# Block-sparse attention with global keys, fused with a cosine MLP: blocks of 48 queries instead of 56, wrapped first keys, global rows gathered by heads, and a new order of the first loads

## The chip, the cores and the metric

The kernel runs on one core of a Trainium2 chip. Its engines are TensorE (PE in the profile, with the weight loads listed apart as PEld), VectorE (DVE), ScalarE (ACT), GpSimd (POOL) and SyncE (SP), and 16 DMA engines. SP and POOL issue all DMAs here: SP's go through the queue q1 (hardware_dynamic), POOL's through q0 (software_dynamic). The metric is the device time of one execution in microseconds (us). Before the change the median of three runs is 395.34 us (395.01 to 399.19). "Faster" and "slower" are told against that median.

## The reference, cut to what matters

Attention over 8 batches x 8 heads, 576 positions, 64 dimensions. A query sees the keys within 32 positions and 8 global keys; the 8 global queries see every key. Its output, turned to 4608 tokens x 512, goes through an MLP with h * cos(h).

```python
scores = (q @ k.T) / sqrt(64)
mask = (abs(pos_i - pos_j) <= 32) | is_global[i] | is_global[j]
attn = softmax(where(mask, scores, -1e9))
x = (attn @ v)                    # [8, 8, 576, 64] -> [4608, 512]
h = x @ w_in                      # 512 -> 2048
out = (h * cos(h)) @ w_out        # 2048 -> 512, float32
```

## The kernel before, in words

**Tiling of the attention.** Two heads of one batch form a pair; there are 32 pairs. For each pair the 576 queries are cut into NB = 11 blocks of QB = 56. A block works on W = 120 window keys (32 ahead of the block, the block, 32 behind) and G = 8 global keys, 128 keys in all, and on C = 64 query columns for each head: 8 global queries and 56 of its own. Eleven blocks of 56 are 616 queries, so the last block runs past the end, and the first one begins 32 keys before it; both take zeros there.

- `kw` holds the keys of a pair, [128 dims of two heads, 11, 128 keys]; `qb` the queries, [128, 11, 2 heads, 64], with zeros in the other head's half, so that one matmul gives both heads. `vw` holds the values, [128 keys, 11, 2, 65], the 65th column being ones for the sum of the softmax. `kw` and `qb` have 4 buffers each, `vw` has 4.
- `scores(pr, g)`: four blocks (three for g = 2): matmuls of keys (stationary, 128 columns) with queries (128 columns) into PSUM (L440), exponential on ACT (L442), product with the mask on DVE (L443).
- `values(pr)`: 22 matmuls (L452), stationary the 64 columns of `pm` for one block and head, moving the 65 columns of `vw`; even and odd blocks go to PSUM rows 0 to 63 and 64 to 127. Then the sums and the normalised rows (L457 to L463) on DVE.
- `turn_x(pr)`: six transposes (L475), then DVE copies the block rows into `xT` (L478), and after the fourth pair of a batch POOL copies the global rows (L483).

**Loads.** `cast_half(s)` writes the float32 inputs of half a batch (4 heads, two pairs) to float16 copies in DRAM (`v16`, `k16`, `q16`). `load_v(pr)` then reads windows of `v16` into `vw`: one DMA for each head over 120 partitions and 11 blocks, in 128-byte pieces, cut apart where the read would pass the end of the tensor. `load_vg(pr)` (L316) copies the 8 global value rows to all 11 blocks, a DMA for each head that reads the same 64 elements 11 times. For the first eight pairs keys and queries come by `load_qk` straight from float32 and are turned by PE (`turned`, L407); for the rest `turn_half` reads `k16` and `q16` with DMA transposes (L265, L266).

**Global rows.** `gather(src, dst, half)` fetches the global rows of q, k or v for half of the batches with two indirect DMAs; `build_globals(half)` turns keys and queries (ACT, PE, ACT) and copies the values to float16. It is called for the first half at the start and for the second after step 5; the second six gathers are issued in step 4.

**MLP.** `one()` issues a group of 4 matmuls of `w_in` (L491), cosine on ACT (L494), product on DVE (L495); `two()` issues 4 matmuls with `w_out` (L505), and every fourth time the copy out and a store.

**Order.** Everything is in an order written out by hand (`manual_schedule`): each engine runs its instructions in program order. First comes a preamble, then the string FRONT (pairs 0 to 3 and the loads for what follows), then steps s = 2 to 15. Step s works on pairs 2s and 2s+1 along the string ORDER (THIRD for s = 2) with letters for scores (s), values (p), turn_x (x), local keys and queries of the next pairs (k, q), casts (G), squares for a later check (n), and the MLP groups (1, 2). At the end of a step SP is given `turn_half(s + 2)` and the value loads of pairs 2s+4 and 2s+5. Then a tail runs what is left of the MLP.

The lines that the prediction's steps touch are the ones above and, in the preamble, the memsets of `kn` and `qn` (L600), `qb` (L615, L629) and `vw` (L616 to L619), the mask (L326 to L367), and the load of `w_out` (L686).

Of the kernel before, what the change touches and what calls it, by code (L numbers as in the profile page):

```python
# [21 lines left out]
QB = 56  # L22
NB = 11
G = 8
W = 120
BP = 6
KL = 32
HY = 4
RW = 8
KPAD = 4  # L30
KP = KPAD + S // RW + 10
QP = S // RW + 6
KT = KL + S + 80
QT = S + 48
# [6 lines left out]
ORDER = "sa0 sa1 sa2 2 2 2 sz0 2 sz1 sz2 pa 1 1 2 xa pz G 1 1 2 xz n 1 1 2 kc qc 1 kd qd 2 1"  # L41

THIRD = "sa0 sa1 sa2 sz0 sz1 sz2 1 1 pa 1 1 xa pz G 1 1 kc qc xz 1 1 kd qd 1 n 1"

FRONT = ("s0.0 s0.1 s0.2 s1.0 s1.1 s1.2 k2 q2 g4 L2 p0 k3 q3 s2.0 s2.1 s2.2 g5 W0 c2 p1 x0 g6 W1 s3.0 s3.1 s3.2 g7 I "
         "p2 x1 L3 v4 v5 p3 x2 k4 q4 x3 W2 k5 q5 n0 W3 c3 v6 v7")
# [145 lines left out]
def kernel(  # L192
# [22 lines left out]
    ident16 = const.tile([P, P], FP16)  # L215
    pio2 = const.tile([P, 1], FP32)
# [7 lines left out]
    nc.sync.dma_start(gidx_col, dview(gi, 0, (0, 16), (2, G), (1, 1)))  # L224
    nc.sync.dma_start(gidx_all, dview(gi, 0, (0, P), (1, 2 * G)))
    nc.sync.dma_start(gidx_row, dview(gi, 0, (2 * G, 1), (1, 2 * G)))
# [9 lines left out]
    qT = [keep.tile([P, 2, QT], FP16, name=f"qT{i}") for i in range(2)]  # L236
    kn = [keep.tile([KP, 2 * 2, RW, D], FP16, name=f"kn{i}") for i in range(2)]
    qn = [keep.tile([QP, 2 * 2, RW, D], FP16, name=f"qn{i}") for i in range(2)]
    vw = [keep.tile([P, NB, 2, D + 1], FP16, name=f"vw{i}") for i in range(NV)]
    NK = 4  # L240
    kw = [keep.tile([P, NB, P], FP16, name=f"kw{i}") for i in range(NK)]
# [14 lines left out]
    def load_qk(s):  # L256

        base = s * 4 * S * D
        for src, dst in ((k, kn[s % 2][KPAD : KPAD + S // RW]), (q, qn[s % 2][0 : S // RW])):
            nc.gpsimd.dma_start(dst.rearrange("x h r d -> x h (r d)"),  # L260
                                dview(src, base, (RW * D, S // RW), (S * D, 4), (1, RW * D)))

    def turn_half(s):

        nc.sync.dma_start(kT[s % 2][:, :, KL : KL + S], k16[s], transpose=True)  # L265
        nc.sync.dma_start(qT[s % 2][:, :, 0:S], q16[s], transpose=True)  # L266


    qg32 = keep.tile([P, 2, 2, D], FP32)
    kg32 = keep.tile([P, 2, 2, D], FP32)  # L270
    vg32 = keep.tile([P, 2, 2, D], FP32)
# [6 lines left out]
    def index_rows():  # L278

        g_i = work.tile([P, 1], I32, tag="g_i", bufs=1)  # L280
        nc.vector.tensor_scalar(g_i, p_i, G - 1, None, ALU.bitwise_and)
        p8 = work.tile([P, 1], FP32, tag="p8", bufs=1)
        nc.vector.scalar_tensor_tensor(p8, g_i, -1.0, p_i, ALU.mult, ALU.add)
        nc.vector.scalar_tensor_tensor(gidx_rows, p8, float(2 * S // G), gidx_col, ALU.mult, ALU.add)

    def gather(src, dst, half):
        rows = src.rearrange("b h s d -> (b h s) d")
        for h in range(2):
            nc.gpsimd.indirect_dma_start(
                out=dst[:, half, h], out_offset=None, in_=rows,  # L290
                in_offset=bass.IndirectOffsetOnAxis(ap=gidx_rows[:, 0:1], axis=0),
                element_offset=(half * 32 + h) * S * D)

    vg16 = keep.tile([P, 2, 2, D], FP16)

    def load_v(pr):


        b, h0 = pr // NP, 2 * (pr % NP)
        vt = vw[pr % NV]  # L300
        for h in range(2):
            lo, i0, i1 = (b * H + h0 + h) * S * D, 0, NB
            if pr == 0 and h == 0:
                nc.sync.dma_start(vt[G + 32 : P, 0, h, 0:D], dview(v16, 0, (D, W - 32), (1, D)))
                i0 = 1
            if pr % 2 and h:

                nc.sync.dma_start(vt[G : G + 104, NB - 2, h, 0:D], dview(v16, lo + 472 * D, (D, 104), (1, D)))  # L308
                nc.sync.dma_start(vt[G : G + 48, NB - 1, h, 0:D], dview(v16, lo + 528 * D, (D, 48), (1, D)))
                i1 = NB - 2  # L310
            nc.sync.dma_start(vt[G:P, i0:i1, h, 0:D],
                              dview(v16, lo + (QB * i0 - 32) * D, (D, W), (QB * D, i1 - i0), (1, D)))

    def load_vg(pr):
        for h in range(2):
            nc.sync.dma_start(  # L316
                vw[pr % NV][0:G, :, h, 0:D],
                view(vg16[(pr % 16) * G : (pr % 16 + 1) * G, pr // 16, h], (0, NB), (1, D)))


    mask = keep.tile([P, NB, 2, C], FP16)

    def build_mask():
# [24 lines left out]
        nc.vector.tensor_scalar(own, df[:, 0:1], float(W), None, ALU.is_lt)  # L348
        nc.vector.memset(own[0:G], 0.0)
        for h in range(2):  # L350
            nc.vector.tensor_tensor(
                mask[:, :, h, G:], view(nk, (1, NB), (0, QB)), view(band[:, G:], (0, NB), (1, QB)), ALU.mult)
            nc.vector.tensor_scalar(
                mask[:, :, h, 0:G], view(val, (1, NB), (0, G)), own[:, 0:1], None, ALU.mult)
# [18 lines left out]
    def build_globals(half):  # L373
        for src, dst in ((kg32, kgT), (qg32, qgT)):
            g16 = work.tile([P, P], FP16, tag="g16")
            nc.scalar.copy(g16, src[:, half].rearrange("x h d -> x (h d)"))
            t = ps.tile([P, 16 * G], FP16, tag="s", bufs=3)
            nc.tensor.transpose(t, g16, ident16)
            nc.scalar.copy(dst[:, 16 * half : 16 * half + 16], t.rearrange("x (n g) -> x n g", g=G))
        nc.scalar.copy(vg16[:, half], vg32[:, half])  # L380
# [4 lines left out]
    xT = keep.tile([P, NC, NT + 40], FP16)  # L385
# [15 lines left out]
    def turned(src, pr, n):  # L401

        t = ps.tile([P, RW, n], FP16, tag="h" if front[0] else "s", bufs=2 if front[0] else 3)
        h0 = 2 * (pr % 2)
        for r in range(RW):
            for h in range(2):
                nc.tensor.transpose(t[h * D : (h + 1) * D, r], src[:n, h0 + h, r], ident16[:n, :n])  # L407
        return t

    def local_k(pr):  # L410
        to = kw[pr % NK][:, :, G:]
        if pr < 2 * HY:
            t = turned(kn[pr // 2 % 2], pr, KP)
            nc.scalar.copy(view(to, (P, NB), (RW, W // RW), (1, RW)),  # L414
                           view(t, (QB // RW, NB), (1, W // RW), (KP, RW)))
        else:
            nc.vector.tensor_copy(to, view(kT[pr // 2 % 2][:, pr % 2], (QB, NB), (1, W)))

    def local_q(pr):
        if pr < 2 * HY:  # L420
            t = turned(qn[pr // 2 % 2], pr, QP)
        for h in range(2):
            hp = slice(h * D, (h + 1) * D)
            to = qb[pr % NK][hp, :, h, G:]
            if pr < 2 * HY:
                copy = nc.scalar.copy if h == 0 or pr < 2 else nc.vector.tensor_copy
                copy(view(to, (2 * C, NB), (RW, QB // RW), (1, RW)),
                     view(t[hp], (QB // RW, NB), (1, QB // RW), (QP, RW)))
# [3 lines left out]
    def scores(pr, g):  # L432
        kp, qp = kw[pr % NK], qb[pr % NK]
        if g == 0:
            pm_of[pr] = work.tile([P, NB, 2, C], FP16, tag="pm", name="pm")
        pm = pm_of[pr]
        g0, n = 4 * g, min(4, NB - 4 * g)
        st = ps.tile([P, 4, P], FP32, tag="s", bufs=3)
        for j in range(n):
            nc.tensor.matmul(st[:, j], kp[:, g0 + j], view(qp[:, g0 + j], (1, P)), start=True, stop=True)  # L440
        e = work.tile([P, 4, P], FP16, tag="e", bufs=3)
        nc.scalar.activation(e[:, :n], st[:, :n], AF.Exp, scale=scale)  # L442
        nc.vector.tensor_tensor(  # L443
# [317 lines left out]
```

## Time and profile before

| what | value |
| --- | --- |
| median of three runs | 395.34 us |
| the profiled execution's own time | 397.13 us |
| its span, first to last instruction | 395.4 us |
| PE, DVE, ACT, POOL busy | 328.3, 260.6, 238.8, 114.8 us |
| MLP matmuls (L491, L505) | 142.8 and 140.4 us, 576 each |
| scores matmuls (L440), values matmuls (L452) | 30.8 us x352, 20.6 us x704 |
| DMA packets | 188504, of which 177005 under 512 B |
| first scores matmul | 20.86 us |
| first MLP matmul (L491) | 59.42 us |
| first scores matmul of steps 2, 3, 4, 5, 6, 7, 8, 9, 10 | 55.46, 74.98, 99.68, 118.22, 140.05, 157.00, 175.37, 192.29, 209.20 us |

The profile is one execution. In the row of 40 slices each slice is 9.9 us, a digit is the busy share in tenths. A row of a timeline gives the start, the length, the engine and line, the operation, and in brackets how long the engine had stood idle and what ended it. "SPq" and "POOLq" are the queues' own work: issuing a DMA. A landing time is that of the last completion event of a DMA in the trace. Matmuls are pipelined, so that a row's length overlaps the next one; what a matmul occupies is read from the distance of two starts.

### The profile page before, as it was taken

The numbers are of one execution on the slowest core, as the hardware profiler recorded it, in microseconds if no ns is written. First come the engines' busy times: TensorE is split into PE (matmuls) and PEld (weight loads), VectorE is DVE, ScalarE is ACT, GpSimd is POOL, SyncE is SP. The second block draws the span as 40 slices with busy tenths as digits, with TensorE's granted clock in tenths as the row PEclk, the third lists the DMA queues.
The fourth block names the chain that finished last, engine by engine and source line by source line (L and its number), as shares of the span: only waits on it lengthen the run. The fifth ranks groups of instructions, "written<-read, shape, count | busy, mean of one in ns | idle before, by whom it ended". The sixth has DMA issues, their size and how long they took to land.

```text
span 395.4 us, 7373 instructions
## 1 busy us (share of the span) xinstructions
PE 328.3 (83%) x2678; PEld 174.7 (44%) x2678; DVE 260.6 (66%) x600; ACT 238.8 (60%) x351; POOL 114.8 (29%) x250
## 2 busy tenths in 40 slices
PE   0272179576778889899999999999999979999993
PEld 0262164343434355455555555555555334444441
DVE  7744157555687768789788888888889354544300
ACT  1572066945575686677778678776777866244210
POOL 6573032504268275071443507223000100000000
PEclk9997558969999999999999999999999999999999
DMA  6989979999999999999999999999990000010121
GB/s 92 96 123 199 123 43 181 215 130 124 176 121 177 108 175 131 166 154 180 149 176 187 127 177 140 191 141 120 144 118 31 27 2 27 28 54 27 55 80 60
DMA packets 188504, 47.18 MB, mean 119 GB/s; under 512 B 177005, under 2 KB 183405, under 8 KB 188205
## 3 DMA queue, kind: packets, MB, share of 16 engines
q1 hardware_dynamic: 124509, 27.89, 59.6%
q0 software_dynamic: 63952, 18.75, 48.4%
q8 instruction: 23, 0.38, 0.5%
q14 instruction: 20, 0.16, 0.2%
HBM read 47.73 MB, written 21.23 MB: 174 GB/s over the span
## 4 chain that ended last, share of the span: by engine, by line
PE 67%; DMA 10%; DVE 8%; ACT 5%; issue 3%; SPq 3%; another core or an unknown queue 1%; POOL 0%; ACTq 0%; DVEq 0%
PE po L505 28%; PE ph L491 27%; DMA q<-in_q_dram 4%; PE st L440 4%; PE pv L452 4%; DMA vw<-vg 3%; DMA vw<-v 3%; DVE g L495 2%; PE tx L475 2%; SPq L308 2%; ACT cos L494 2%; DVE xn L463 1%; PE t L407 1%; ACT sq L524 1%
## 5 line engine op out<-in xcount | busy, mean ns | idle before, releaser
L491 PE MATMUL ph<-xT,w_in 128*128 128x512 f16 x576 | 142.8, 385 | 6.7 <-DVE g L495 5.9
L505 PE MATMUL po<-w_out,g 128*128 128x512 f16 x576 | 140.4, 380 | 5.0 <-DMA w_out<-in_moe_w_out_dram 3.6
L494 ACT ACTIVATE cos<-ph,pio 128x512 f16<-128x512 f32 x144 | 97.3, 686 | 77.2 <-PE ph L491 75.6
L495 DVE TENSOR_TENSOR g<-cos,ph 128x512 f16<-128x512 f16 x144 | 96.4, 685 | 55.0 <-ACT cos L494 52.7
L505 PEld LDWEIGHTS <-g 128*128 128x128 f16 x576 | 55.4, 98 | 67.7 <-issue 5.2
L491 PEld LDWEIGHTS <-w_in 128*128 128x128 f16 x576 | 54.1, 99 | 69.4 <-issue 13.1
L442 ACT ACTIVATE e<-st 128x512 f16<-128x512 f32 (+1 forms) x96 | 47.6, 561 | 14.3 <-PE st L440 9.3
L443 DVE TENSOR_TENSOR pm<-e,mask 128x512 f16<-128x512 f16 (+1 forms) x96 | 37.0, 405 | 23.8 <-ACT e L442 21.9
L662 POOL COPY gate<-xn 1x1 f16<-1x1 f16 x14 | 2.5, 182 | 143.3 <-DVE xn L463 143.3
L452 PE MATMUL pv<-vw,pm 128*64 128x65 f16 x704 | 20.6, 204 | 23.1 <-issue 10.3
L440 PE MATMUL st<-qb,kw 128*128 128x128 f16 x352 | 30.8, 238 | 4.2 <-ACT e L442 1.5
L440 PEld LDWEIGHTS <-kw 128*128 128x128 f16 x352 | 26.3, 108 | 14.2 <-POOL xT L483 2.9
L463 DVE TENSOR_TENSOR xn<-pv,r_all 128x768 f16<-128x768 f32 x32 | 30.6, 958 | 1.9
L452 PEld LDWEIGHTS <-pm 128*64 128x64 f16 x704 | 16.6, 117 | 27.3 <-issue 19.0
L253 POOL DMA_DIRECT2D q<-in_q_dram x12 | 27.6, 2304 | 0.0
L414 ACT COPY kw<-t 128x1320 f16<-128x1320 f16 x8 | 10.1, 1257 | 28.7 <-PE t L407 28.7
L483 POOL COPY xT<-xg 128x4 f16 x64 | 20.5, 320 | 22.0 <-DVE xT L478 18.6
L510 ACT COPY o<-po 128x512 f32<-128x512 f32 x18 | 10.5, 586 | 22.4 <-PE po L505 21.9
L524 ACT ACTIVATE sq<-xn 128x1536 f16<-128x1536 f16 x16 | 23.6, 1474 | 0.0
L430 DVE COPY qb<-qT 64x616 f16<-64x616 f16 x48 | 22.1, 460 | 0.3
L253 POOL DMA_DIRECT2D k<-in_k_dram x12 | 21.2, 1765 | 0.3 <-issue 0.3
L512 DVE COPY o<-po 128x512 f32<-128x512 f32 x18 | 12.3, 685 | 12.1 <-PE po L505 12.0
(106 smaller groups left out, 269.2 us busy)
## 6 DMA issues: line engine op xcount, KB each, us to landing
out_dram<-o SPq DMA_DIRECT2D x36, 256.0 KB
vw<-v SPq DMA_DIRECT2D x47, 165.0 KB
v<-in_v_dram POOLq DMA_DIRECT2D x16, 288.0 KB
k<-in_k_dram POOLq DMA_DIRECT2D x12, 288.0 KB
q<-in_q_dram POOLq DMA_DIRECT2D x12, 288.0 KB
vw<-v SPq DMA_DIRECT2D x16, 135.0 KB
w_in<-in_moe_w_in_dram POOLq DMA_DIRECT2D x4, 512.0 KB
w_out<-in_moe_w_out_dram POOLq DMA_DIRECT2D x1, 2048.0 KB
```

Of the source, the lines that this page charges most:

```text
L253: nc.gpsimd.dma_start(dst[s].rearrange("t (h d) -> t h d", h=4), dview(src, base, (D, S), (S * D, 4), (1, D)))
L430: nc.vector.tensor_copy(to, view(qT[pr // 2 % 2][hp, pr % 2], (QB, NB), (1, QB)))
L440: nc.tensor.matmul(st[:, j], kp[:, g0 + j], view(qp[:, g0 + j], (1, P)), start=True, stop=True)
L442: nc.scalar.activation(e[:, :n], st[:, :n], AF.Exp, scale=scale)
L443: nc.vector.tensor_tensor(view(pm[:, g0], (1, n * P)), view(e, (1, n * P)), view(mask[:, g0], (1, n * P)), ALU.mult)
L452: nc.tensor.matmul(pv[r0 : r0 + C, j // 6, c0 : c0 + 65], pm[:, j, h], vp[:, j, h], start=True, stop=True)
L463: nc.vector.tensor_tensor(view(xn, (384, 2), (D, 6), (1, D)), view(pv, (512, 2), (65, 6), (1, D)), view(rp, (6, 2), (1, 6), (0, D)), ALU.mult)
L491: nc.tensor.matmul(ph, w_in16[:, j, f * P : (f + 1) * P], xT[:, j, t * TT : (t + 1) * TT], start=(j == 0), stop=(j == NC - 1))
L494: nc.scalar.activation(cos, ph, AF.Sin, bias=pio2)
L495: nc.vector.tensor_tensor(g16[:, f], cos, ph, ALU.mult)
L505: nc.tensor.matmul(po, g16[:, f, s * P : (s + 1) * P], w_out16[:, f], start=(f == 0), stop=(f == NF - 1))
L524: nc.scalar.activation(sq, view(xn, (1, 2 * BP * P)), AF.Square, accum_out=x_sq[:, s : s + 1])
```

## The change

Blocks become 48 queries: NB = 12, W = 112 window keys, KW = 120 keys with the global ones, C = 56 query columns for each head. Twelve blocks of 48 are the 576 queries, so nothing runs past the end. The first block takes the sequence's last 32 keys where it took zeros; the mask drops them as before. The padding and zeroing of `kn`, `qn`, `qT`, `xT` go. `vw` is laid out by head, then by block. `load_v` loads block 0 of both heads with two DMAs of its own (80 and 32 partitions) and the other blocks with one for each head over 112 partitions.

Global rows are gathered for 16 heads of the flattened list at a time, three indirect DMAs (k, q, v) for eight pairs, four times in all: in the preamble and in steps 2, 6 and 10, ahead of the casts. `vgw` holds the global values spread to all 12 blocks, one buffer; `spread_globals` writes it on ACT and `load_vg` copies contiguous 780-element rows of it. New letters in ORDER and THIRD: `b` copies gathered rows (ACT) and `t` turns and spreads them (PE, ACT).

The start is put in another order: the loads of `kn` and `qn` first, `qb` zeroed by ACT copies, the gathers of k and q ahead of the first cast of v, values of pairs 2 and 3 loaded ahead of the first part of `w_in`, `w_in`'s third and fourth parts ahead of the last `turn_x`, and `w_out` in four parts at the end of FRONT.

```diff
-QB = 56
-NB = 11
+QB = 48
+NB = 12
 G = 8
-W = 120
+W = 112
+KW = G + W
...
-ORDER = "sa0 sa1 sa2 2 2 2 sz0 2 sz1 sz2 pa 1 1 2 xa pz G 1 1 2 xz n 1 1 2 kc qc 1 kd qd 2 1"
-THIRD = "sa0 sa1 sa2 sz0 sz1 sz2 1 1 pa 1 1 xa pz G 1 1 kc qc xz 1 1 kd qd 1 n 1"
-FRONT = ("s0.0 s0.1 s0.2 s1.0 s1.1 s1.2 k2 q2 g4 L2 p0 k3 q3 s2.0 s2.1 s2.2 g5 W0 c2 p1 x0 g6 W1 s3.0 s3.1 s3.2 g7 I "
-         "p2 x1 L3 v4 v5 p3 x2 k4 q4 x3 W2 k5 q5 n0 W3 c3 v6 v7")
+ORDER = "sa0 sa1 sa2 2 2 2 sz0 2 sz1 sz2 pa 1 1 2 xa pz G 1 1 2 xz n 1 1 2 kc qc 1 b kd qd 2 t 1"
+THIRD = "sa0 sa1 sa2 sz0 sz1 sz2 1 1 pa 1 1 xa pz G 1 1 kc qc xz 1 1 b kd qd 1 n t 1"
+FRONT = ("g0 s0.0 s0.1 s0.2 c1 k1 q1 g1 B s1.0 s1.1 s1.2 v2 v3 g2 g3 W0 L2 c2 k2 q2 p0 s2.0 x0 s2.1 s2.2 W1 I "
+         "k3 q3 p1 s3.0 x1 s3.1 s3.2 L3 c3 g4 g5 k4 q4 p2 v4 v5 W2 x2 p3 W3 k5 q5 x3 n0 v6 v7 g6 g7 O0 O1 O2 O3")
...
-    vw = [keep.tile([P, NB, 2, D + 1], FP16, name=f"vw{i}") for i in range(NV)]
+    vw = [keep.tile([P, 2, NB, D + 1], FP16, name=f"vw{i}") for i in range(NV)]
-    kw = [keep.tile([P, NB, P], FP16, name=f"kw{i}") for i in range(NK)]
+    kw = [keep.tile([P, NB, KW], FP16, name=f"kw{i}") for i in range(NK)]
...
+    def gather(src, dst, n):
+        nc.gpsimd.indirect_dma_start(
+            out=dst, out_offset=None, in_=src.rearrange("b h s d -> (b h s) d"),
+            in_offset=bass.IndirectOffsetOnAxis(ap=gidx_rows[:, 0:1], axis=0),
+            element_offset=n * 2 * GP * S * D)
+    vgw = keep.tile([P, NB, D + 1], FP16)
+    def load_v(pr):
+        vt, n0, p0 = vw[pr % NV], 2 * pr * S * D, G + KL
+        nc.sync.dma_start(vt[p0:KW, :, 0, 0:D], dview(v16, n0, (D, W - KL), (S * D, 2), (1, D)))
+        nc.sync.dma_start(vt[G:p0, :, 0, 0:D], dview(v16, n0 + (S - KL) * D, (D, KL), (S * D, 2), (1, D)))
+        for h in range(2):
+            lo, i1 = n0 + (h * S - KL) * D, NB
+            if pr % 2 and h:
+                i1 = NB - 1
+                nc.sync.dma_start(vt[G : KW - KL, h, i1, 0:D], dview(v16, lo + QB * i1 * D, (D, W - KL), (1, D)))
+            nc.sync.dma_start(vt[G:KW, h, 1:i1, 0:D], dview(v16, lo + QB * D, (D, W), (QB * D, i1 - 1), (1, D)))
     def load_vg(pr):
         for h in range(2):
-            nc.sync.dma_start(
-                vw[pr % NV][0:G, :, h, 0:D],
-                view(vg16[(pr % 16) * G : (pr % 16 + 1) * G, pr // 16, h], (0, NB), (1, D)))
+            p0 = (pr % GP * 2 + h) * G
+            nc.sync.dma_start(vw[pr % NV][0:G, h], vgw[p0 : p0 + G])
...
+    def copy_globals(which):
+        for x in which:
+            g16 = g16_of[x] = work.tile([P, 2, D], FP16, tag="g16", name="g16")
+            nc.scalar.copy(g16, view({"k": kg32, "q": qg32}[x], (0, 2), (1, D)))
+    def turn_globals(which, n):
+        for x in which:
+            t = ps.tile([P, GP, 2, G], FP16, tag="s", bufs=3)
+            nc.tensor.transpose(t.rearrange("x n h g -> x (n h g)"), g16_of.pop(x).rearrange("x h d -> x (h d)"), ident16)
+            for h in range(2):
+                hp = slice(h * D, (h + 1) * D)
+                nc.scalar.copy({"k": kgT, "q": qgT}[x][hp, GP * n : GP * (n + 1)], t[hp, :, h])
+    def spread_globals():
+        nc.scalar.copy(vgw[:, :, 0:D], view(vg32, (0, NB), (1, D)))
...
     def local_k(pr):
...
+            nc.gpsimd.tensor_copy(to[:, 0, 0:KL], to[:, NB - 1, W - 2 * KL : W - KL])
         else:
-            nc.vector.tensor_copy(to, view(kT[pr // 2 % 2][:, pr % 2], (QB, NB), (1, W)))
+            kt = kT[pr // 2 % 2]
+            if pr % 2 == 0:
+                nc.vector.tensor_copy(kt[:, :, 0:KL], kt[:, :, S : S + KL])
+            nc.vector.tensor_copy(to, view(kt[:, pr % 2], (QB, NB), (1, W)))
...
     with tc.manual_schedule():
+        nc.sync.dma_start(gidx_col, dview(gi, 0, (0, 2 * GP), (2, G), (1, 1)))
+        nc.sync.dma_start(gidx_all, dview(gi, 0, (0, P), (1, 2 * G)))
+        nc.gpsimd.iota(p_i, pattern=[[0, 1]], base=0, channel_multiplier=1)
+        load_qk(0)
...
-        for t in (kn[0], qn[0], kn[1], qn[1]):
-            nc.vector.memset(t, 0.0)
+        for i in range(NK):
+            nc.vector.memset(kw[i][:, NB - 1, KW - KL :], 0.0)
+            nc.scalar.copy(view(qb[i], (1, NB * 2 * C)), view(zero16, (0, NB * 2 * C)))
...
         gather(k, kg32, 0)
         gather(q, qg32, 0)
+        cast_half(0, "v")
         gather(v, vg32, 0)
         load_qk(1)
-        cast_half(1, "v")
+        copy_globals("k")
+        local_k(0)
+        copy_globals("q")
+        turn_globals("kq", 0)
+        build_mask()
+        local_q(0)
         load_v(0)
         load_v(1)
...
+        def first_globals(_):
+            spread_globals()
+            load_vg(0)
+            load_vg(1)
...
             nc.gpsimd.tensor_copy(gate, xn_of[s][0:1, 1, 0, 0:1])
+            if s % 4 == 2 and s // 4 < 3:
+                for src, dst in ((k, kg32), (q, qg32), (v, vg32)):
+                    gather(src, dst, s // 4 + 1)
             for n in range(4, 2 * B):
                 if s == (n - 2 if n < 7 else n - 3):
                     cast_half(n, "vkq")
-            if s == 4:
-                for src, dst in ((k, kg32), (q, qg32), (v, vg32)):
-                    gather(src, dst, 1)
...
-            if s == 2:
-                nc.gpsimd.dma_start(w_out16, moe_w_out.rearrange("(c p) n -> p c n", p=P))
...
+                elif step in "bt":
+                    if s % 4 == 2 and s // 4 < 3:
+                        if step == "b":
+                            copy_globals("kq")
+                        else:
+                            turn_globals("kq", s // 4 + 1)
+                            spread_globals()
...
-            if s == 5:
-                build_globals(1)
```

## The prediction

> **What bounds the kernel now.** I read the 40 slices first, then PE's busy time by stage, then the timeline where PE stands still.
>
> ```profile
> PE   0272179576778889899999999999999979999993
> PEclk9997558969999999999999999999999999999999
> DMA  6989979999999999999999999999990000010121
> ```
>
> PE is full only from about slice 17; before that it waits, and twice its clock is halved (slices 4 to 5, part of 8). The DMA engines are busy to 90% nearly everywhere up to slice 30. A stage of one step in the later part:
>
> ```profile
> 181.00:198.00 17.00, 17.00 (x144) 9.08 (x142) 14.67 (x34) 12.99 (x21) 5.48 (x10) 1.00 1.60 166
> ```
>
> PE is busy for all 17.00 us, VectorE for 14.67, ScalarE for 12.99. Steps start every 16.92 us here (175.37, 192.29, 209.20), so from step 8 on PE sets the pace. Earlier steps are longer: step 2 lasts 19.5, step 3 24.7, step 4 18.5, step 5 21.8, step 7 18.4 us. These rows say why:
>
> ```profile
> 79.32 1.49 PE L505 MATMUL po<-w_out,g 128*128 128x512 f16 x4 [3.57 <-DMA w_out<-in_moe_w_out_dram]
> ...
> 91.61 0.76 PE L452 MATMUL pv<-vw,pm 128*64 128x65 f16 x22 [3.03 <-DMA vw<-v]
> ...
> 139.16 0.23 PE L378 MATMUL t<-ident,g 128*128 128x128 f16 x1 [0.97 <-ACT g L376]
> ...
> 166.56 0.76 PE L452 MATMUL pv<-vw,pm 128*64 128x65 f16 x22 [1.19 <-DMA vw<-vg]
> ```
>
> Each stall hangs on a DMA: `w_out`, values of pair 7, the second gathers, the global values of pair 15. So the change is worth what it does to landings up to step 7, plus any wait it adds in steps that are full.
>
> **The sum's base.** The profiled execution took 397.13 us, 1.7 around a span of 395.4; the median is 395.34. I work with differences and add them to the median.
>
> **PE in full steps.** Eleven scores matmuls of 128 columns take 0.61 us (192.29 to 192.90), 55.5 ns each. Twelve of 112 columns take 12 x 48.5 = 0.58 if the columns set the pace. But weights shrink from 128 columns to 120, and the rows say that narrower is not quicker:
>
> ```profile
> L440 PEld LDWEIGHTS <-kw 128*128 128x128 f16 x220 | 14.8, 98 | 6.8
> L452 PEld LDWEIGHTS <-pm 128*64 128x64 f16 x418 | 8.7, 110 | 3.3 <-DMA vw<-vg 1.4
> ```
>
> 64 columns take 110 ns, 128 take 98. Starts in `values` lie 29 and 35 ns apart in each half of the array, so a 64-column load fits into 29 ns, and 120 columns at that rate into 54: 12 x 54 = 0.65. I take 0.62. `values` goes from 22 matmuls in 0.50 us to 24, at 23 ns each, 0.545. Per step of two pairs +0.1 us; for steps 4 to 15 **+1.2** (0 to 1.8). The exponentials (1344 for 1408 columns), mask products and copies get shorter, the wrap copy of 64 elements on VectorE costs some 0.1 us; both engines have over 2 us free in 17, so all this is nothing.
>
> The Trainium skill, "TensorE: Matmul & The Clock Gate", section on Fast Weight Load, has the fast load only at exactly 128 weights, and its LDWEIGHTS section gives columns / 1.2 ns, an estimate of 100 ns for 120 columns. By that the scores would take 1.2 us a pair. The trace's 64 columns in 29 ns (that formula: 53) speak against the figure, not against the rule.
>
> **Loads.** Landing events show how a DMA is divided: loads of 120 partitions end with 15 completions on the engines, those of 104 with 13, the global values (8 partitions) with 8. A head was 1320 pieces over 15 engines, 88 each; now 112 partitions suit 16 engines, 77 each and 7 for block 0. The global values go from 88 pieces to 8 rows. From landings where one queue ran alone, two pairs of values took 6.8 us (49.77 to 56.53), 3.4 each; now 3.1. Against that a step has 13 value DMAs for 10 on SP, at 0.3 to 0.7 us of issue; SP has room.
>
> **The start.** Before, `kn`'s load is issued at 2.38, behind a memset, and lands at 8.39; the index rows are ready at 5.69. Now the load goes at about 1.05, the rows are ready at 4.7 (`gidx_col` lands at 4.01), `kn` lands at 7.1 and the first gathers at 9.2 behind `qn`. ScalarE's four zero copies (1344 elements at the 0.96 ns of the 1536-element square: 1.3 us each) end at 7.5, in a gap. Then copies and transposes, 3.8 us by the old rows: first scores at 13.2 for 20.86. This doesn't carry: `values` of pair 0 waits for `vw`, whose global rows lie in q1 behind pair 1's values; 22.5 for 26.22. Next, `w_in`'s first part and the second `kn` are issued at about 20 (27.34 and 25.09 before) and share the engines with pairs 2 and 3.
>
> Work alone, from landings: `kn` or `qn` 1.6, a cast of v 0.9, a quarter of `w_in` 2.6, `w_out` 10.4 to 11.5, a gather 0.5. Up to `w_out` and the values of pair 7 that is 8 x 3.1 + 12.8 + 3.6 + 1.5 + 10.4 + 10.4 = 63.5; two queues together ran at 0.95 of the sum of such times (14.4 in 15.3 us, 26.5 to 41.8), so 67 us from 5.4: both land at 72, for 79.28 and 91.79. The first MLP matmul comes at about 50 for 59.42.
>
> **Step 2, a new wait.** The gathers of the second group are now issued behind `w_out` on q0. Before, gathers issued at 120.82 landed at 134.14, 0.3 us behind the cast queued ahead; so the queue keeps order, and these land at 71 to 73. ScalarE stands at `b` for them, and at `t` for another thing: `spread_globals` overwrites `vgw`, so it waits until `load_vg` of pair 7 has landed, also 72. Behind it on ScalarE lie a cosine, the table load and the exponentials of step 3. From 71: copies 0.6, `kw` 1.4, `qb` 0.65, cosine 0.7, squares 1.7, turned rows 0.9, spread 0.83, cosine 0.7, table 1.3: exponentials at 80, step 3 as if from 79.2 (74.98 before). But step 3 then has `w_out` and its values, and takes 17 to 19 for 24.7. Step 4 starts at 98: **-1.5** (-7 to +5).
>
> **Steps 4 and 5** lose 1.6 and 4.9 us over 16.92 before; the six gathers and their ScalarE waits leave step 5, while `qT`, landing at 135.84 behind two rounds of casts, stays: **-4.3** (-6 to 0).
>
> **Steps 6 and 10, the same wait.** `spread_globals` there needs the values issued at the end of the step before. This is how the end of step 10 looks:
>
> ```profile
> 222.51 2.48 SPq L316 DMA_DIRECT2D vw<-vg  x2
> ...
> 225.46 0.59 ACT L510 COPY o<-po 128x512 f32<-128x512 f32 x1 [0.17 <-PE po L505]
> ...
> 226.32 0.69 ACT L494 ACTIVATE cos<-ph,pio 128x512 f16<-128x512 f32 x1 [0.28 <-PE ph L491]
> ```
>
> The spread sits between that copy and that cosine. The global rows issued at 222.51 and 224.29, of pair 23, land at 231.35, 22.2 us after their step's end (209.20); pair 15's landed 26.7 after. Shorter loads take 1.4 off: 230. Then spread 0.83, cosine 0.69, table 1.28, exponential 0.6: PE's next scores group at 233.4 for 229.33. PE covers the first part with one MLP group and three `two` groups, which 229.33 already counts. **+4** in step 10 (+2 to +5.4). In step 6 the lag of 26.7 would cost 8.5, one of 22.2 4.0; I take **+6**, for the queues get time to catch up in step 2's wait. Pair 15's stall of step 7 goes: **-1.4**.
>
> **Sum.** -1.5 - 4.3 + 6 + 4 - 1.4 + 1.2 = +4.0: **399.5 us**. A measurement of this kernel tells about 1% from no change (4 us).
>
> **Rivals.**
> 1. Not slower: the values land before ScalarE comes to the spread. It needs a lag of 17 us or less after the step's end where 22.2 to 26.7 were measured; for it speaks that in steps 6 and 10 gathers of 4 us of issue push the casts back, which compete with these loads. It takes away the +10 and leaves 1 us of ScalarE work: 390.5.
> 2. The engines give q0 the turn: between 31.7 and 41.3 pair 2's second head took 9.6 us for 1.6 of work beside `w_in`. With `w_in` and `kn` issued 5 to 7 us earlier the first values come later (pair 0 at 29), `w_out` and pair 7 at 80, step 4 at 104: 405.
> 3. Weights of 120 columns load at 100 ns, in PE's path: 12 x 100 - 611 = 0.59 us a pair, 24 pairs in full steps, +14: 413. Nothing in a row asks for it; no row has 120 columns.
> 4. The early start isn't there: ScalarE stood 3.2 us at 11.3 for a PE event that came late; if such a wait returns, step 2 starts as before and only the spread's cost is left: 401.
>
> **Chances.** Forecast 0.42 (own range 394 to 404), rivals 0.20, 0.22, 0.06, 0.10. Below 391.4: most of rival 1 and a little of the forecast, 0.18. Above 399.3: half of the forecast and most of 2, 3, 4, 0.50. Between: 0.32. The range, 8 in 10, is 389 to 408.
>
> **What would show it.** First scores near 13 and first MLP matmul near 50; `w_out` and pair 7 landing near 72; ScalarE idle before the line of `spread_globals`, released by a `vw<-vgw` DMA, for several us in steps 2, 6 and 10, and those steps 4 to 8 us longer than 16.92, others 16.9 to 17.1; twelve scores matmuls in 0.58 to 0.65 us. I am wrong if ScalarE reaches the spread with the DMA long landed, or if steps 8, 9 and 11 to 15 grow by more than 0.2 us.

## The result: 1.0066 of before, near the forecast, by a partly different road

| what | before | after |
| --- | --- | --- |
| median of 20 runs each | 396.88 us (393.72 to 400.30) | 399.08 us (396.11 to 402.77) |
| profiled execution, own time / span | 397.13 / 395.4 us | 397.23 / 395.5 us |
| PE, DVE, ACT, POOL busy | 328.3, 260.6, 238.8, 114.8 us | 330.8, 254.7, 247.0, 120.1 us |
| q0 and q1, share of 16 engines | 48.4%, 59.6% | 48.1%, 45.1% |
| first scores matmul / first MLP matmul | 20.86 / 59.42 us | 15.11 / 58.52 us |

The ratio is 1.0066 with a 95% interval of 1.0037 to 1.0095: 2.6 us longer, less than the 1% that was taken as the bound of "same". The forecast was 399.5 us. The profiled execution of after is one of its shorter ones, 1.85 us under its median; that of before lies 0.25 us over its own. So the two spans are nearly equal although the medians are not, and the traces show the parts of the change better than their sum.

The starts of the steps (first scores matmul) in both profiles, in us:

| step | 2 | 3 | 4 | 5 | 6 | 7 | 8 | 10 | 11 | 12 | 15 |
| --- | --- | --- | --- | --- | --- | --- | --- | --- | --- | --- | --- |
| before | 55.46 | 74.98 | 99.68 | 118.22 | 140.05 | 157.00 | 175.37 | 209.20 | 226.12 | 243.04 | 293.79 |
| after | 53.68 | 80.09 | 99.24 | 118.26 | 135.26 | 153.44 | 173.43 | 207.39 | 225.13 | 242.74 | 293.67 |
| difference | -1.8 | +5.1 | -0.4 | 0.0 | -4.8 | -3.6 | -1.9 | -1.8 | -1.0 | -0.3 | -0.1 |

Steps 4 and 5 win 4.4 us (the differences at 4 and 6), and steps 6, 7, 10 and 11 give back 4.4. The 40 slices of after, 9.9 us each:

```profile
PE   0373169479779997899999999999999879999993
PEclk9999999869999999999999999999999999999999
DMA  5999969986999999999999899997820000010121
```

Counted from 0, PE still starves up to slice 8, and slices 7 and 8 now have the lowered clock. A full step (columns: the stretch, its length, busy time of PE, PEld, DVE, ACT, POOL, granted clock, DMA share, GB/s):

```profile
181.00:198.00 17.00, 17.00 (x150) 9.30 (x149) 14.12 (x35) 12.87 (x20) 5.62 (x10) 1.00 1.42 177
...
215.00:232.00 17.00, 16.25 (x146) 8.61 (x144) 14.99 (x33) 13.33 (x26) 8.86 (x13) 1.00 1.03 127
```

PE sets the pace as before; the second row has the end of step 10 and the start of step 11, where it idles 0.75 us. The waits of ScalarE, by the timeline of ACT in after (in brackets the idle time before the row and what ended it):

```profile
76.41 0.30 ACT L368 CAST g<-kg 128x128 f16<-128x128 f32 x1 [2.84 <-DMA kg<-in_k_dram,gidx_rows]
...
81.64 0.83 ACT L379 CAST vgw<-vg 128x768 f16<-128x768 f32 x1
...
156.13 0.83 ACT L379 CAST vgw<-vg 128x768 f16<-128x768 f32 x1 [2.41 <-DMA vw<-v]
...
225.43 0.83 ACT L379 CAST vgw<-vg 128x768 f16<-128x768 f32 x1
```

The spread (L379) is there three times. In step 2 it follows a wait, but that wait is for the gathers behind `w_out`; pair 7's global rows landed at 75.95, before the spread's turn. In step 6 it waits 2.41 us for pair 15's global rows, which land at 155.74 and 155.95 (landing events and rows agree to some 0.2 us). In step 10 it waits for nothing. What PE has of it:

```profile
76.76 0.29 PE L373 MATMUL t<-ident,g 128*128 128x128 f16 x1 [2.70 <-ACT g L368]
...
159.68 0.40 PE L447 MATMUL st<-qb,kw 128*120 128x112 f16 x4 [2.83 <-ACT e L449]
```

### The profile page after: what moved, and what is told of

It is laid out like the page before. It is cut to its first block, busy times and chain, and to the rows that moved or that the text cites. A ratio compares the mean times of both kernels' runs of the same rounds, so it can differ in the third digit from the quotient of the medians.

```text
span 395.5 us, 7721 instructions
## 1 busy us (share of the span) xinstructions
PE 330.8 (84%) x2778; PEld 178.2 (45%) x2778; DVE 254.7 (64%) x605; ACT 247.0 (62%) x379; POOL 120.1 (30%) x261
## 3 DMA queue, kind: packets, MB, share of 16 engines
q0 software_dynamic: 64000, 18.75, 48.1%
q1 hardware_dynamic: 122722, 28.28, 45.1%
## 4 chain that ended last, share of the span: by engine, by line
PE 67%; ACT 11%; issue 8%; DMA 5%; DVE 5%; POOL 1%; SPq 1%; ACTq 0%; POOLq 0%; DVEq 0%
PE po L511 28%; PE ph L497 28%; PE st L447 4%; DMA kg<-in_k_dram,gidx_rows 4%; PE pv L458 3%; ACT cos L500 3%; PE tx L481 2%; DVE g L501 2%; ACT kw L414 2%; ACT e L449 1%; ACT sq L530 1%; DVE xn L469 1%; ACT L449 1%; DMA vw<-vgw 1%; DMA gidx_col<-in_global_idx_dram 1%
## 5 line engine op out<-in xcount | busy, mean ns | idle before, releaser
L497 PE MATMUL ph<-xT,w_in 128*128 128x512 f16 x576 | 144.3, 388 | 6.9 <-DVE g L501 5.0
L501 DVE TENSOR_TENSOR g<-cos,ph 128x512 f16<-128x512 f16 x144 | 96.9, 685 | 59.6 <-ACT cos L500 57.6
L449 ACT ACTIVATE e<-st 120x448 f16<-120x448 f32 x96 | 46.3, 544 | 20.7 <-PE st L447 18.3
L450 DVE TENSOR_TENSOR pm<-e,mask 120x448 f16<-120x448 f16 x96 | 37.4, 393 | 21.8 <-ACT e L449 18.8
L447 PE MATMUL st<-qb,kw 128*120 128x112 f16 x384 | 33.1, 236 | 15.1 <-ACT e L449 4.8
L447 PEld LDWEIGHTS <-kw 128*120 128x120 f16 x384 | 31.9, 152 | 24.6 <-issue 12.3
L458 PE MATMUL pv<-vw,pm 120*56 120x65 f16 x768 | 20.2, 203 | 11.6 <-DMA vw<-v 10.7
L489 POOL COPY xT<-xg 128x4 f16 x64 | 22.1, 345 | 8.4 <-DVE xT L484 4.8
L516 ACT COPY o<-po 128x512 f32<-128x512 f32 x18 | 10.5, 585 | 22.2 <-PE po L511 22.0
L530 ACT ACTIVATE sq<-xn 128x1536 f16<-128x1536 f16 x16 | 23.6, 1474 | 0.0
L458 PEld LDWEIGHTS <-pm 120*56 120x56 f16 x768 | 16.3, 113 | 15.3 <-issue 11.2
L481 PE MATMUL tx<-ident,xn 128*128 128x128 f16 x192 | 17.3, 231 | 5.9 <-DVE xn L469 5.2
L481 PEld LDWEIGHTS <-xn 128*128 128x128 f16 x192 | 13.6, 103 | 13.9 <-DVE xn L469 8.4
```

The lines of the kernel that those rows point to most:

```text
L447: nc.tensor.matmul(st[:, j], kp[:, 4 * g + j], view(qp[:, 4 * g + j], (1, 2 * C)), start=True, stop=True)
L449: nc.scalar.activation(e, st, AF.Exp, scale=scale)
L450: nc.vector.tensor_tensor(view(pm[:, 4 * g], (1, n)), view(e, (1, n)), view(mask[:, 4 * g], (1, n)), ALU.mult)
L458: nc.tensor.matmul(pv[r0 : r0 + C, j // 6, c0 : c0 + 65], pm[:, j, h], vp[0:KW, h, j], start=True, stop=True)
L481: nc.tensor.transpose(tx[:, n], xn[:, n], ident16)
L497: nc.tensor.matmul(ph, w_in16[:, j, f * P : (f + 1) * P], xT[:, j, t * TT : (t + 1) * TT], start=(j == 0), stop=(j == NC - 1))
```

## The experiments

Each kernel was timed beside the kernel before on the same chip; ratios are to that (its median lay between 394.29 and 396.97 us there, so ratios are compared and not times). After stands at 1.0066.

### 1. Two buffers for the spread: the wait in step 7

```diff
-    vgw = keep.tile([P, NB, D + 1], FP16)
+    vgw = [keep.tile([P, NB, D + 1], FP16, name=f"vgw{i}") for i in range(2)]
...
-            nc.sync.dma_start(vw[pr % NV][0:G, h], vgw[p0 : p0 + G])
+            nc.sync.dma_start(vw[pr % NV][0:G, h], vgw[pr // GP % 2][p0 : p0 + G])
...
-        nc.scalar.copy(vgw[:, :, 0:D], view(vg32, (0, NB), (1, D)))
+        nc.scalar.copy(vgw[n % 2][:, :, 0:D], view(vg32, (0, NB), (1, D)))
```

> Two vgw tiles, used in turn by the groups of eight pairs, so that spread_globals waits for no load_vg. In the trace of after the only long wait of ScalarE before that line is 2.41 us until 156.13, and behind it PE stands 2.83 us at 159.68. By the trace this run is 2.8 us shorter than after, so 0.999 to 1.000 of before, and step 7 lasts 17 us instead of 20. By the prediction's prices (6 us in step 6 and 4 in step 10) it is 10 us shorter, 0.981 of before. If something else is late at the same place (the cosine, the table load), it stays at 1.0066.

Measured: 0.993 (0.9885 to 0.9975), 1.36% less than after, 5.4 us, with about 2 us of uncertainty from the two intervals. In the profile step 7 lasts 17.61 us for 19.99, and the spread (154.77) comes without a wait. That is 2.4 us of the gain; the trace is of one of this kernel's longer executions (397.13 us; its median is 393.76), and it doesn't show the rest. So the wait is real and its removal alone takes the change below before. The gain lies between the two prices that were expected.

### 2. The gathers earlier: a gain in step 2, and a loss that shows the price of the wait

```diff
-            if s % 4 == 2 and s // 4 < 3:
-                for src, dst in ((k, kg32), (q, qg32), (v, vg32)):
-                    gather(src, dst, s // 4 + 1)
+            if s % 4 == 1 and 1 < s < 10:
+                gather_group(s // 4 + 1)
...
-... v6 v7 g6 g7 O0 O1 O2 O3
+... v6 v7 g6 g7 A1 O0 O1 O2 O3      (A: gather_group, the same three gathers)
```

> The three gathers of group 1 are issued ahead of w_out, those of groups 2 and 3 one step earlier (steps 5 and 9 instead of 6 and 10); the single vgw stays. Theory: ScalarE's 2.84 us until 76.41 goes, step 3's first scores come at 77 to 78 instead of 80.3, step 10 loses its 0.7 us, step 6 its 1.3, but there the spread is only reached sooner and still waits for pair 15's values. Together 2.5 to 4 us less than after: 0.997 to 1.000 of before. Rival: the first stage is bound by the sum of its transfers, the gathers only push w_out and pair 7's values back by 1.5 us and step 4 starts at 99.5 as before: 1.005.

Measured: 1.0365 (1.0311 to 1.042), against both expectations. Up to step 7 it went as the theory had it: step 2 lasts 22.5 us for 26.4, step 7 starts at 147.3 for 153.4. Then steps 7 and 11 last 26.4 and 26.5 us. The timelines of ACT and PE in this run:

```profile
154.50 0.83 ACT L379 CAST vgw<-vg 128x768 f16<-128x768 f32 x1 [6.87 <-DMA out_dram<-o]
```

```profile
158.05 0.62 PE L447 MATMUL st<-qb,kw 128*120 128x112 f16 x4 [7.30 <-ACT e L449]
158.46 1.91 PE L511 MATMUL po<-w_out,g 128*128 128x512 f16 x4
```

The releaser named there is a store of `out`; what the spread needs, pair 15's global rows, lands at 154.32, 24.9 us after step 6 began (20.7 in after). GpSimd's queue says why. In after, the gathers stand ahead of step 6's casts and hold these back by some 3.5 us (issued from 150.63), and pair 15's loads (issued 148.9 to 152.2) are mostly through before these move. Here the gathers hold back the casts of step 5, on which SP's transposes and, behind these, the loads of pairs 14 and 15 depend, and step 6's casts (issued from 141.13) run beside these loads.

The four matmuls of `po` in the second row take 1.91 us where they take 1.03 elsewhere: the granted clock in the stretch from 156 to 160 is 0.50. So a wait of 7.3 us cost 9.4.

### 3. Both together

The edits of 1 and 2.

> Early gathers as in the run before (ahead of w_out, and in steps 5 and 9 ahead of the casts) together with two vgw tiles. In that run steps 7 and 11 lasted 26.4 us because ScalarE stood 6.87 us before the spread while pair 15's values landed at 154.4. Theory: the spread's wait for vgw alone made that; with two tiles steps 7 and 11 last 17.0 to 17.6 and the run is 19 us shorter than with early gathers alone and 3 to 5 us shorter than with two tiles alone: 0.980 to 0.986 of before. Rival: the casts pushed back by the gathers make the values or qT themselves late; then steps 7 and 11 stay at 20 or more and the run is at 1.00 or above.

Measured: 0.9812 (0.9772 to 0.9852), 388.0 us. Steps 7 and 11 last 17.62 and 17.61 us, though step 5's casts go out as late as in experiment 2 (15.4 to 17.2 us into the step) and pair 15's rows land even later, 26.1 us after step 6 began. So the wait for `vgw` alone made that loss, and late casts did no other harm.

### 4. Weights of 128 columns again

```diff
-    kw = [keep.tile([P, NB, KW], FP16, name=f"kw{i}") for i in range(NK)]
+    kw = [keep.tile([P, NB, P], FP16, name=f"kw{i}") for i in range(NK)]
...
+            nc.vector.memset(kw[i][:, :, KW:], 0.0)
...
-        st = ps.tile([KW, 4, 2 * C], FP32, tag="s", bufs=3)
+        st = ps.tile([P, 4, 2 * C], FP32, tag="s", bufs=3)
```

> kw gets 128 columns instead of 120, the last eight zero, so that the weights of scores are 128 columns wide; the product has 8 rows more, which nobody reads. In after twelve such matmuls start 54 ns apart and a full step lasts 16.98 us. Theory of the prediction: the narrower weights set that pace; with 128 columns it is the 112 columns of the moving operand, 48.5 ns, 24 x 5.5 ns less a step, 16.85, over twelve steps 1.6 us less than after: 1.0025 of before. Rival: 54 ns has another cause, and nothing changes (16.98, 1.0066). If weights of 120 columns cost 100 ns in TensorE's path after all, it would be 14 us less, 0.97.

Measured: 1.0021 (0.9981 to 1.0062); full steps last 16.86 us for 16.98. The groups of lines of PEld between 130 and 300 us, first after, then this run (count, busy us, mean ns):

```profile
L447 PEld LDWEIGHTS <-kw 128*120 128x120 f16 x240 | 17.7, 135 | 9.8 <-issue 3.3 <-POOL qb L398 0.9
L458 PEld LDWEIGHTS <-pm 120*56 120x56 f16 x456 | 8.5, 106 | 1.5
```

```profile
L447 PEld LDWEIGHTS <-kw 128*128 128x128 f16 x240 | 14.6, 98 | 11.8 <-issue 3.8 <-POOL qb L398 1.4
```

120 columns take 135 ns, 128 take 98. In the timeline twelve scores matmuls take 0.65 us in after (242.74 to 243.39) and 0.59 here (243.38 to 243.97). The step is 0.12 us shorter, as the theory had it (0.13); the ratio alone, with its interval, would not have shown that.

### 5. `w_in` later

```diff
-... g2 g3 W0 L2 c2 k2 q2 p0 s2.0 x0 s2.1 s2.2 W1 I k3 q3 p1 s3.0 x1 s3.1 s3.2 L3 c3 g4 g5 k4 q4 p2 v4 v5 W2 x2 p3 W3 k5 ...
+... g2 g3 L2 c2 k2 q2 p0 s2.0 x0 s2.1 s2.2 W0 I k3 q3 p1 s3.0 x1 s3.1 s3.2 L3 c3 W1 g4 g5 k4 q4 p2 v4 v5 x2 p3 W2 W3 k5 ...
```

> w_in's four parts each go later into GpSimd's queue: the first behind the second scores of pair 2, the second behind the casts of that stage, the last two behind the third values. Nothing else changes. If the early parts of w_in took the engines from the values of pairs 2 and 3 (rival 2), these land at 34 to 37 and at 43 to 46 instead of 41.9 and 50.1, and the first MLP matmul comes at 50 to 54 instead of 58.5. If that gain is kept to the end, the run is 5 us shorter than after, 0.994 of before. If the stage up to step 3 is bound by what lands last (w_out and the gathers behind it, 76.4), step 3 starts at 80 all the same and the run is at 1.003 to 1.007.

Measured: 1.0075 (1.0035 to 1.0115), as after. Its profile is of one of its longest executions (406.42 us), so only the first landings are read from it: pair 2's values at 36.20 instead of 41.68, but pair 3's at 52.11 instead of 49.89, for GpSimd's queue has nothing between `W1` and `W3` that waits for more than 1.5 us, and the last parts still went out at 40.90 and 41.64, beside pair 3. `w_in` does take the engines from the values; moved in this way it takes them from other values. The Trainium skill, "DMA: Bandwidth & Descriptors", section "Queues, rings and completion order", has each DMA engine turn round-robin between the queues that have work for it; these landings agree.

### 6. Before, with its six gathers in step 2

```diff
+            if s == 2:
+                for src, dst in ((k, kg32), (q, qg32), (v, vg32)):
+                    gather(src, dst, 1)
...
-            if s == 4:
-                for src, dst in ((k, kg32), (q, qg32), (v, vg32)):
-                    gather(src, dst, 1)
```

> The kernel before, with one thing moved: the six gathers of the second half are issued in step 2 instead of step 4; build_globals(1) stays at the end of step 5. The prediction puts the shorter steps 4 and 5 (4.3 us) down to these gathers. Theory: steps 4 and 5 together last 36 instead of 40.4 us, and the run is 3.5 to 5 us shorter than before, 0.987 to 0.991. Rivals: qT and the casts are as late as they were, and the gain is 0 to 1 us (0.998 to 1.000); or the gathers push the casts of step 2 back and steps 3 and 4 lose what step 5 gains (1.00).

Measured: 0.9893 (0.9852 to 0.9934), 4.2 us less than before, the size expected, but it doesn't lie where it was expected: against before, steps 3, 5 and 7 are 1.6, 2.9 and 1.45 us shorter, steps 4 and 6 1.5 and 1.2 longer. Step 5 still lasts 18.9, for `build_globals` still makes PE wait 1.5 us there. In step 4 twelve matmuls of `po` take 4.38 us for 2.75: the granted clock is 0.74 between 98 and 102. So steps 4 and 5 together are only 1.4 us shorter than before, and the drop of the clock took another 1.6 from them.

### 7. Only the first gathers early, and the others behind the casts

Both have two `vgw` and group 1's gathers ahead of `w_out`. In the first, groups 2 and 3 stay in steps 6 and 10; in the second they go behind the casts of steps 5 and 9:

```diff
                     cast_half(n, "vkq")
+            if s % 4 == 1 and 1 < s < 10:
+                gather_group(s // 4 + 1)
```

> Two vgw tiles, and only the gathers of group 1 moved ahead of w_out; those of groups 2 and 3 stay behind the gate of steps 6 and 10, ahead of that step's casts. Expected: step 2 as with early gathers (22.5 us instead of 26.4), step 6 and 10 with ScalarE's wait for the gathers as in after (1.2 to 1.9 us each), step 7 near 17.6: 3.5 to 4.5 us less than two tiles alone, 0.982 to 0.985 of before. Rival: w_out and pair 7's values, now behind the gathers, take the place of the wait, and step 4 starts at 99 to 100 as in after: 0.993.

> Two vgw tiles, gathers of group 1 ahead of w_out, those of groups 2 and 3 in steps 5 and 9, but behind that step's casts in GpSimd's queue, so that they push no cast back and have landed before ScalarE asks for them. Expected: steps 6, 7, 10 and 11 at 17.0 to 17.3, 3 us less than with the gathers of these groups in steps 6 and 10: 0.974 to 0.978 of before. If the place of the gathers to the casts matters nothing once vgw is double, it equals the run with both changes within 0.3%.

Measured: 0.9882 (0.9841 to 0.9923) and 0.984 (0.9788 to 0.9892). The first gained less than was expected (0.982 to 0.985). In its profile step 2 lasts 20.86 us and step 4 starts at 94.9 for 100.1 with two tiles alone: `w_out` and pair 7, now behind the gathers, didn't take the wait's place. In the second, steps 7, 10 and 11 last 17.6, 17.5 and 17.6 us, not 17.0 to 17.3, and step 6 lasts 18.9, with a new wait of 1.18 us for a `vw<-vgw` load. So a place behind the casts is no better than one ahead of them in step 5 (experiment 3): the intervals overlap, 0.3% apart.

### 8. Global values in pieces of 128 bytes

```diff
-            nc.sync.dma_start(vw[pr % NV][0:G, h], vgw[p0 : p0 + G])
+            nc.sync.dma_start(vw[pr % NV][0:G, h, :, 0:D], vgw[p0 : p0 + G, :, 0:D])
```

> The kernel after, with load_vg written as 8 x 12 pieces of 128 bytes a head, as the kernel before has 8 x 11, instead of 8 rows of 1560 bytes. In after the global values of pair 23 land 16.5 us after the start of their step instead of the 22.2 of before, so that ScalarE meets no wait in step 10. Theory: that is because the gathers now stand ahead of that step's casts, and the loads escape these; then pieces change little, the load lands within 1.5 us of 224.1 and the run is 0 to 2 us longer than after, 1.007 to 1.012 of before. Rival: the fewer, longer pieces made the loads quick; then pair 23 lands at 227 or later, step 7 lasts 22 to 25 us, steps 10 and 11 4 us longer, and the run is 4 to 8 us longer than after, 1.017 to 1.027.

Measured: 1.0206 (1.0154 to 1.0257), the rival's time, 5.5 us more than after. But the landings side with the theory in step 10: pair 23's land 17.5 us after the start of their step (16.5 in after), and steps 10 and 11 are 0.5 us longer together. The loss is in step 7. ACT's and PE's timelines, and the windows (columns as above):

```profile
158.89 0.83 ACT L379 CAST vgw<-vg 128x768 f16<-128x768 f32 x1 [4.74 <-DMA vw<-vgw]
```

```profile
162.43 0.62 PE L447 MATMUL st<-qb,kw 128*120 128x112 f16 x4 [5.16 <-ACT e L449]
```

```profile
157.00:161.00 4.00, 0.27 (x2) 0.00 (x0) 0.53 (x1) 2.07 (x3) 0.00 (x0) 1.00 1.89 225
161.00:164.00 3.00, 1.57 (x7) 0.90 (x8) 1.67 (x5) 2.62 (x5) 0.00 (x0) 0.62 1.46 136
164.00:167.00 3.00, 3.00 (x36) 2.05 (x35) 1.91 (x7) 1.79 (x3) 0.00 (x0) 0.50 1.45 140
```

Pair 15's rows land 23.6 us after step 6 began for 20.7, the spread waits 2.3 us more than in after, and step 7 lasts 25.2 us, 5.2 more: the clock is at half behind the wait. The rival had step 7 at 22 to 25 us by a later landing; the clock neither had, and why the pieces cost 2.9 us at the landing in step 6 but 1.0 in step 10 is open. q1's time rises from 178.4 us (0.451 x 395.5) to 185.3 (0.461 x 401.9).

### 9. Half of `w_out`

```diff
-... g6 g7 O0 O1 O2 O3
+... g6 g7 O0 O1
...
+        nc.vector.memset(w_out16[:, NF // 2 :], 0.0)
```

> The kernel after with the second half of w_out not loaded (those weights are zero instead, so half of the second product's sum is left out; the instructions stay). 5.2 us of transfers less ahead of the gathers of group 1. Theory: the first stage ends with the sum of its transfers, so the gathers land at about 71.5 instead of 76.6, step 3 starts at 75 to 76 instead of 80.3, and the run is 4 to 5 us shorter than after: 0.994 to 0.997 of before. Rival: the stage is held by the engines (values of pairs 2 and 3, copies); then step 3 starts at 79 to 80 and the run stays at 1.004 to 1.007.

Measured: 1.0013 (0.997 to 1.0056), 2.1 us less than after with about as much uncertainty. The gathers and step 3 went as the theory had it; ACT's timeline:

```profile
72.14 0.30 ACT L368 CAST g<-kg 128x128 f16<-128x128 f32 x1 [0.90 <-DMA kg<-in_k_dram,gidx_rows]
```

Step 3 starts at 76.0 for 80.1, step 4 at 94.8 for 99.2: 4.1 and 4.4 us, most of the 5.2 us of the transfers. By step 15 the lead is 2.6. Step 7 lost 1.7 of it: PE's wait is 3.02 us for 2.83, and behind it the clock falls to 0.50 (between 157.5 and 160).

### 10. All three, and the spread on GpSimd

The edits of 1, 2 and 4; then, on top, for groups 1 to 3:

```diff
-        nc.scalar.copy(vgw[n % 2][:, :, 0:D], view(vg32, (0, NB), (1, D)))
+        copy = nc.gpsimd.tensor_copy if n else nc.scalar.copy
+        copy(vgw[n % 2][:, :, 0:D], view(vg32, (0, NB), (1, D)))
```

> Two vgw tiles, the early gathers (group 1 ahead of w_out, groups 2 and 3 in steps 5 and 9) and kw of 128 columns, all at once. If the three act on different things they add up: 0.9812 with the first two, 0.0045 less for the third, 0.977 of before (0.973 to 0.981), a full step 16.86 us. If a shorter step runs into another bound (transfers that were just in time), it is 0.981 or more.

> As the run with all three changes, and the spreads of groups 1 to 3 done by GpSimd instead of ScalarE. In the runs without waits steps 7 and 11 still last 17.6 us for 16.98, because ScalarE has 0.83 us of spread ahead of the cosine, the table load and the exponentials, and PE waits 0.44 us for these. Expected: steps 7 and 11 at 16.9 to 17.0, 1.2 us less: 0.974 of before. Rival: GpSimd takes some 2 us for it and holds up its own kw and qb copies, no gain: 0.977.

Measured: 0.9863 (0.9816 to 0.9909), 389.0 us, and 0.9809 (0.9758 to 0.9861), 387.75 us, both above what was expected (0.977 and 0.974). The first didn't add up in time, though its full steps are 16.86 us: in its profile steps 3 and 4 are 1.5 us longer each than in experiment 3. In step 4 PE's two waits are 0.90 and 1.00 us, as there (0.90 and 0.92), but here the clock is 0.64 between 92 and 96 and there it is 1.00. Step 3's 1.5 us are left open. With the spread on GpSimd steps 7 and 11 last 16.86 us, no longer than the others (step 6 lasts 19.6 there, 1.43 of it a wait for a `vw<-vgw` load). GpSimd takes longer for it than ScalarE's 0.83 us:

```profile
145.07 1.94 POOL L380 CAST vgw<-vg 128x768 f16<-128x768 f32 x1
```

It beats both kernels, as experiment 3 does (0.9812); between the two the intervals can't tell.

## Why the prediction was right, and where it was not

The time came out (399.5 forecast, 399.08 measured), the sum less so. The forecast added 4.0 us to the median of three runs, 395.34; twenty runs put before at 396.88 and the change at 2.2 to 2.6 us. So it is in part luck that 399.5 lies so near: the base was 1.5 us too low and the change 1.4 to 1.8 too large. Against the profile, where they add to -0.1 at the start of step 15, the terms are:

| term | forecast | profile of after | what the runs say |
| --- | --- | --- | --- |
| start and steps 2, 3 | -1.5 | -0.4 | transfers end the stage (experiment 9) |
| steps 4, 5 | -4.3 | -4.4 | right size; gathers alone 4.2 in all, 1.4 of it here (experiment 6) |
| steps 6 and 7 | +6 - 1.4 | +2.9 | right kind; two tiles give 5.4 in the median (experiment 1) |
| steps 10 and 11 | +4 | +1.5 | no wait; casts held back (experiments 2, 7, 8) |
| PE in full steps | +1.2 | +0.3 (steps 8, 9, 12 to 14, 0.06 each; the others have it in their rows) | right kind (experiment 4) |

- **PE in full steps.** Scores took 0.65 us, the upper of the two bounds, where 0.62 was taken; the 24 matmuls of `values` took 0.49 (181.80 to 182.29), no more than the 22 before, where 0.545 was taken. PE stayed the bound. Rival 3, weights at 100 ns in PE's path, is out: 14 us were foreseen, and 128 columns gave 0.12 us a step.
- **Loads.** 3.1 for 3.4 us a pair was far too small a gain: q1's time fell from 235.7 us (0.596 x 395.4) to 178.4, a quarter. The whole rows in `load_vg` are 6.9 us of the 57 (experiment 8); that the rest comes from 16 engines for 15 was only argued. The number of packets fell by 1% (124509 to 122722). By the packets in the traces, one of 128 bytes took 26 ns before, 18 in after and 19 in experiment 8; and one of 256 bytes, which the DMA transposes move and the change leaves as they were, fell from 34 to 27. So this time also holds something other than a load's own work, and no run here parts the two.
- **The start.** First scores at 15.11 (13.2 was forecast) and pair 0's values at 23.37 (22.5) were near. The first MLP matmul was not: 58.52 where 50 was said. Rival 2 had the reason: `w_in` and the keys issued early delay pairs 2 and 3, whose values land at 41.68 and 49.89 (experiment 5). But the rival's time, 405, was wrong with it, because the stage doesn't end there.
- **Step 2.** What ends it was right: ScalarE stands at `b` for gathers behind `w_out`. They landed from 76.4 on for 71 to 73; step 3 began at 80.09 (79.2) and step 4 at 99.24 (98). Half of `w_out` moved all of that 4.1 to 4.4 us forward, so it is transfers that set it. The second wait, for pair 7's rows, was hidden behind the first.
- **Steps 6 and 7.** The wait at the spread came, 2.41 us, and PE lost 2.83. In this execution that is less than the 6 foreseen; the medians of experiment 1 say 5.4. The term lacked a part: a wait near 3 us or longer can cost more than itself, because the clock falls behind it.
- **Steps 10 and 11.** The step that failed is "Shorter loads take 1.4 off: 230". The rows of pair 23 landed at 223.88, 16.5 us after their step's start for 22.2 before. Rival 1 had named the reason: the step's own gathers push its casts back, beside which these loads would run. The two kernels of experiment 7 part this from the loads: both have their loads of step 10 issued from 6 to 14 us into the step, but the first has that step's casts at 15.4 us, behind the gathers, and the second at 11.3; pair 23's rows land at 16.3 and 20.4 us. Where the casts aren't held back and the single tile stays, in experiment 2, step 11 lasts 26.5 us, more than was ever priced. In step 6 the same thing only shortened the wait.

So the new blocks, the loads and the early start, with the wait taken away (0.993), are worth no more than another place for the six gathers of before (0.9893).

Left open is why the median of after lies 1.85 us over its profile. Step 7 stands there at 2.83 us of idle time and kept its clock, and in experiment 9 a wait hardly longer lost it (last section); that other executions of after lose it would explain the median, but only one execution has a trace.

## What to carry to other kernels

A buffer that is refilled once in many steps wants a second copy when its readers are DMAs: the write waits for the last of them, on an engine that others wait for, and here a copy of 1560 bytes a partition gave 1.4%. Price such a wait by what is queued at the readers' landing and not by the loads' own length, for moving three small gathers by one step changed it from none to 7 us. And when PE idles near 3 us in a full stage, count the clock as well.

## What the hardware showed that was not expected

**What a wait of 3 us costs depends on where it falls.** PE's wait ahead of the second scores group of step 7, and by how much the step was longer than a full step of the same kernel (16.98 us, 16.86 with weights of 128 columns):

| run | wait | step longer by | clock behind it |
| --- | --- | --- | --- |
| after | 2.83 us | 3.0 us | 1.00 |
| half of `w_out` | 3.02 us | 4.7 us | 0.50 from 157.5 to 160 |
| weights of 128 columns | 3.33 us | 3.5 us | 1.00 |
| pieces | 5.16 us | 8.2 us | 0.50 from 164 to 167 |
| gathers early | 7.30 us | 9.4 us | 0.50 from 156 to 160 |

The second and the third row in the timelines of PE:

```profile
155.31 0.40 PE L447 MATMUL st<-qb,kw 128*120 128x112 f16 x4 [3.02 <-ACT e L449]
```

```profile
160.31 0.36 PE L447 MATMUL st<-qb,kw 128*128 128x112 f16 x4 [3.33 <-ACT e L449]
```

Where the clock fell the extra is 1.7 to 3.0 us, whatever the wait; where it held, 0.2. The length alone doesn't decide it: 3.02 us lost the clock and 3.33 kept it. In every trace here the granted clock changes only at times that lie a multiple of 3.41 us apart. Laid on that grid, the wait of 3.33 us falls into two cells, which have 1.90 and 1.42 us of idle PE; of the 3.02 us, 2.08 lie in one cell (153.23 to 156.64), and the clock is at half in the next (156.64 to 160.06). In after it is 1.39 and 1.44. Step 4 of experiment 6, with 2.25 us in one cell, lost the clock too. So in these runs 1.90 us of idle time in a cell kept the clock and 2.08 lost it; but one cell with 1.67 lost it as well, so that idle time is not the whole rule. That one is in step 4 of experiment 10, where both waits fall into one cell; in experiment 3 nearly equal waits leave at most 1.08 us in a cell. The Trainium skill, "TensorE: Matmul & The Clock Gate", section "Part 1: The HAM clock gate", has the clock fall to half after an idle window of about 3.4 us and return after as long a busy one, on a window that runs free of the kernel. The grid agrees; that a whole window must be idle does not: 2.08 us of 3.41 were enough.

**The order of two queues' issues in the first stage can differ with the same code up to there.** In after the last part of `w_in` goes out at 38.42, ahead of pair 3's last load (40.27), which lands at 49.89. In experiment 2, the same program up to there, that load goes first (39.77; the last two parts of `w_in` at 40.99 and 41.78) and lands at 45.77. Step 2 then starts at 51.2 instead of 53.7, with no edit that asks for it. In experiment 9, again the same program up to there, the load goes first by only 0.13 us (39.77 and 39.90) and lands at 50.44; step 2 starts at 54.0. So the start of step 2 moves by more than 2 us between single traces, and a smaller difference there shows nothing of an edit.
